# The k^T v product of a linear-attention block: v as the weights, k's softmax divided in place, KV turned by VectorE

## The chip, the cores and the metric

The kernel runs on one core of a Trainium2 chip. The core has five engines that work side by side and wait for each other by semaphores: TensorE (matmuls; in the profile PE, its weight loads PEld), VectorE (DVE), ScalarE (ACT), GpSimd (POOL), and SyncE (SP), which issues most of the transfers. Matmul results land in PSUM, eight banks of 512 fp32 columns on each of 128 partitions; everything else lies in SBUF. The metric is the device time of one execution in microseconds, the median of three timed runs.

## The reference

One transformer block in bfloat16 on 2048 rows of width 640: a linear attention with 32 heads of width 20, then a gated feed-forward layer of width 1536. The part that matters here, cut:

```python
qkv = (x @ wqkv).reshape(B, S, 3, H, Dh)...            # q, k, v per head, Dh = 20
pk = einsum("bhsd,hdf->bhsf", k, w_phi)                # pq from q in the same way
phi_k = concatenate([softmax(pk), softmax(-pk)], -1)   # softmax over the 20 features
kv = einsum("bhsf,bhsd->bhfd", phi_k, v)               # per head, summed over all 2048 rows
z  = einsum("bhsf->bhf", phi_k)
num = einsum("bhqf,bhfd->bhqd", phi_q, kv)
den = einsum("bhqf,bhf->bhq", phi_q, z)[..., None] + 1e-6
o = num / den                                          # then @ wo, residual, feed-forward
```

So each head needs, for each of two signs (the softmax of pk and that of -pk), a 20x20 matrix k^T v and a row z, the sum of phi_k. Nothing of the attention's output can be computed before all 2048 rows of k and v have gone into them.

## The kernel before

The rows are cut into 16 tiles of 128 (a row tile has 128 rows on the partitions). The order of the work on every engine is written out by hand; no scheduler moves anything. Each engine takes its own instructions strictly in the order of the program.

*K phase* (loop over t at line 479, about 17 to 69 us). For each tile: TensorE multiplies the normalised input by the folded k weights (pk, line 288), ScalarE takes exp of pk and of -pk (line 332) into E, a buffer of two halves of 640 columns, one for each sign. TensorE also makes v three tiles ahead (pv), and ScalarE copies it to vS (line 308), where each head has 20 columns of v and a column of ones: the product with the ones gives z. VectorE sums E over each head's 20 features (line 339, `k_norm`) and takes reciprocals rs (line 343). Then v is divided, not k: vt = vS * rs, one instruction for each sign, 128x672 (line 347). The second sign's always runs on GpSimd; the first sign's runs on GpSimd for the tiles listed in `VP` (0, 2, 4, 6, 9, 11, 12) and on VectorE for the others, where it is put off until after the next tile's line 339 (`todo`). There are eight vS buffers, eight E and eight vt.

*k^T v* (`kv_tile`, line 359). The product isn't made tile by tile but in groups, listed in `KVG` and `KVQ`: tiles 0 and 1 in iteration 6, tiles 2 to 5 in iteration 9, tiles 6 to 9 in iteration 13, tiles 10 to 12 in iteration 15 behind the first q products, tiles 13 to 15 after the loop. E is the stationary operand (the weights): for each sign, for each of five chunks of 32 feature columns and each of four quadrants, one weight load of 128x32 and one matmul whose moving operand is vt of the two or three heads that touch the chunk, 42 or 63 columns. The four quadrants are the four blocks of 32 PSUM partitions; matmuls of different quadrants run side by side in the array. That is 40 pairs of weight load and matmul a tile, all adding into one PSUM bank, kvp. As a chunk of 32 features holds parts of two or three heads, the result has blocks that belong to no head.

*The seam* (`kv_mask`, line 370). VectorE adds 0.5e-6 to z (line 372), then multiplies kvp by kmask, which is 1 where a feature row belongs to the head of the column and 0 elsewhere, into KV (line 374). GpSimd builds kmask in iteration 7 (lines 516 to 522), clears KV in iteration 8, and copies kmask into two border columns of KV in iteration 11; SP copies kmask to the other three quadrants with three transfers in iteration 9, ahead of the last load of WqT.

*Q phase* (from line 781). The q products (`q_mm`, line 388; pq, five matmuls of 512 columns for each of 20 chunks) and their exponentials on ScalarE (`q_exp`, line 393, into Eq) are spread over the seam. The attention products (`attn_a`, line 586) use Eq as weights and slices of KV as the moving operand, two or three heads of 22 columns at a time. The first, of tile 0, comes right behind the first half of the fifth q product, and it needs KV. From there each tile goes through VectorE, GpSimd and ScalarE (lines 605 to 640), a transpose oT, the output projection (line 660), a second LayerNorm, and the feed-forward matmuls (lines 720 and 739), which take the rest of the time.

PSUM in this phase is a ring of four double banks (`gtile`); kvp holds one of them from iteration 3 to the seam, and the second q product after the first attention product takes that one over.

## Time and profile before

The three timed runs took 273.31, 273.39 and 273.48 us. The profiled execution of the same program has a span of 272.1 us from its first instruction to its last; what a timed run has beyond that, about 1.3 us, lies before and after.

| what | value |
| --- | --- |
| time, median of 3 runs | 273.39 us |
| span of the profiled execution | 272.1 us |
| TensorE busy | 267.4 us, 98% |
| VectorE / ScalarE / GpSimd busy | 64% / 51% / 37% |
| granted TensorE clock | 0.999 |
| k^T v (line 366) in the chain | 2.2% |
| attention products (line 586) in the chain | 2.3% |
| divisions on GpSimd (line 347) | 23 of 1371 ns |
| divisions on VectorE (line 347) | 9 of 1078 ns |

How to read the lines below: a line of the groups gives source line, engine, operation, output<-inputs, partitions x elements, xcount, then busy time in us and the mean duration of one in ns, then the engine's idle time before them and what ended it. A line of the timeline gives start and length in us, engine, line, operation and count of a run of equal instructions, and in brackets the idle time before it. The length of a run of matmuls includes the last one's way through the array, so the time until the next run's start is what it costs the stream. The chain is the work that ended last, followed back: where it is on TensorE, TensorE was not waiting.

### The profile page before, as it was taken

Reading aid. Unit: us, or ns where it says so; the run is one execution under the profiler, and the core shown is the slowest. Engines: PE = TensorE matmul, PEld = TensorE weight load, DVE = VectorE, ACT = ScalarE, POOL = GpSimd, SP = SyncE. Lnnn points to the kernel's source line nnn. Section 1 sums busy time; section 2 is a strip of 40 time slices with the busy share of each in tenths; the row PEclk is TensorE's granted clock in tenths of the full one; section 3 lists DMA queues with packets and bytes.
Section 4 is the critical chain, followed back from the end, with each engine's and each line's share of the span. In section 5 each row is a group of like instructions: output and inputs, shape, how many; then the busy total and the mean of one; then the engine's idle time right before and its main releaser. Section 6 shows DMA issues by size and latency. Waiting matters only on the chain.

```text
span 272.1 us, 7250 instructions
## 1 busy us (share of the span) xinstructions
PE 267.4 (98%) x2990; PEld 171.9 (63%) x2990; DVE 173.7 (64%) x330; ACT 138.1 (51%) x238; POOL 100.5 (37%) x220
## 2 busy tenths in 40 slices
PE   7999999999999999999999999999999999999996
PEld 6777777765555887788755455675555576444574
DVE  4899999997767766695457874346778332333322
ACT  5669997787789765364624256213345600233100
POOL 4248997877002336374123464003166400000000
PEclk9999999999999999999999999999999999999999
DMA  7987466241676632332202133110222411000011
GB/s 185 213 195 169 69 100 78 51 106 67 224 252 197 197 100 57 75 74 51 57 18 52 25 62 60 48 52 0 51 48 48 52 48 51 24 0 0 2 48 48
DMA packets 45408, 22.11 MB, mean 81 GB/s; under 512 B 37952, under 2 KB 43328, under 8 KB 45376
## 3 DMA queue, kind: packets, MB, share of 16 engines
q1 hardware_dynamic: 44720, 21.64, 33.5%
q8 instruction: 23, 0.38, 0.6%
q10 hardware_dynamic: 656, 0.03, 0.2%
q14 instruction: 9, 0.07, 0.1%
HBM read 10.18 MB, written 2.62 MB: 47 GB/s over the span
## 4 chain that ended last, share of the span: by engine, by line
PE 95%; DMA 2%; ACT 1%; DVE 1%; SPq 0%; issue 0%
PE gu L720 39%; PE pd L739 19%; PE pq L388 8%; PE po L660 8%; PE pk L288 8%; PE pv L288 7%; PE ab L586 2%; PE kvp L366 2%; DMA Wv<-in_A_wqkv_dram 2%; PE wa L240 1%; PE pv L304 1%; ACT vS L308 1%; PE tp L159 0%; DVE LN1T L160 0%; SPq L187 0%
## 5 line engine op out<-in xcount | busy, mean ns | idle before, releaser
L723 ACT ACTIVATE g<-gu 128x512 bf16<-128x512 f32 (+1 forms) x60 | 30.6, 510 | 63.5 <-PE gu L720 62.6
L726 DVE TENSOR_TENSOR GT<-gu,g 128x512 bf16<-128x512 f32 (+1 forms) x60 | 34.3, 578 | 43.8 <-PE gu L720 31.1
L720 PE MATMUL gu<-LN2T,Wg 128*128 128x512 bf16 (+1 forms) x300 | 61.8, 337 | 0.0
L720 PE MATMUL gu<-LN2T,Wu 128*128 128x512 bf16 (+1 forms) x300 | 61.8, 336 | 0.0
L739 PE MATMUL pd<-Wd,GT 128*128 128x320 bf16 (+2 forms) x396 | 53.5, 295 | 0.0
L739 PEld LDWEIGHTS <-GT 128*128 128x128 bf16 x396 | 37.9, 98 | 14.6 <-DVE GT L726 0.2
L720 PEld LDWEIGHTS <-Wu 128*128 128x128 bf16 x300 | 29.4, 98 | 22.6
L720 PEld LDWEIGHTS <-Wg 128*128 128x128 bf16 x300 | 28.6, 98 | 20.3
L288 PEld LDWEIGHTS <-LN1T 128*128 128x128 bf16 x290 | 27.9, 98 | 10.4
L347 POOL TENSOR_TENSOR vt<-vS,rs 128x672 bf16<-128x672 bf16 x23 | 31.0, 1371 | 5.9 <-DVE rs L343 5.7
L742 DVE TENSOR_TENSOR y<-pd,x_sb 128x320 bf16<-128x320 f32 (+2 forms) x29 | 13.9, 480 | 29.4 <-PE pd L739 29.4
L660 PE MATMUL po<-Wo,oT 128*128 128x320 bf16 x160 | 24.5, 299 | 0.0
L288 PE MATMUL pk<-Wk,LN1T 128*128 128x320 bf16 x160 | 24.4, 299 | 0.0
L388 PE MATMUL pq<-LN1T,Wq 128*128 128x512 bf16 x100 | 22.9, 379 | 0.0
L339 DVE TENSOR_REDUCE sk<-E 128x64 f32<-128x1280 bf16 x16 | 22.9, 1429 | 0.0
L393 ACT ACTIVATE Eq<-pq 128x1024 bf16<-128x1024 f32 (+1 forms) x26 | 19.9, 831 | 3.1 <-PE pq L388 3.0
L332 ACT ACTIVATE E<-pk 128x640 bf16<-128x640 f32 x28 | 18.7, 746 | 2.8 <-PE pk L288 2.8
L146 ACT ACTIVATE ln<-x_sb,v,rstd 128x640 bf16<-128x640 bf16 x14 | 12.9, 920 | 14.3 <-POOL v L699 14.2
L660 PEld LDWEIGHTS <-oT 128*128 128x128 bf16 x160 | 15.4, 98 | 6.9 <-ACT oT L160 0.2
L288 PE MATMUL pv<-Wv,LN1T 128*128 128x320 bf16 x130 | 19.8, 299 | 0.0
L635 DVE TENSOR_TENSOR tt<-AB,w 128x1280 bf16<-128x1280 f32 x12 | 17.8, 1486 | 1.0 <-POOL w L628 0.9
L615 POOL TENSOR_TENSOR pr<-AB 128x64 f32<-128x64 f32 x10 | 6.8, 678 | 26.8 <-DVE AB L596 20.7
(114 smaller groups left out, 289.9 us busy)
## 6 DMA issues: line engine op xcount, KB each, us to landing
out_dram<-y SPq DMA_DIRECT2D x15, 160.0 KB, 1.8
x_sb<-in_A_x_dram SPq DMA_DIRECT2D x6, 320.0 KB, 3.4
Wu<-in_B_w_up_dram SPq DMA_DIRECT2D x1, 1920.0 KB, 8.9
Wg<-in_B_w_gate_dram SPq DMA_DIRECT2D x2, 768.0 KB, 5.8
Wd<-in_B_w_down_dram SPq DMA_DIRECT2D x1, 1440.0 KB, 7.8
Wo<-in_A_wo_dram SPq DMA_DIRECT2D x1, 800.0 KB, 4.9
x_sb<-in_A_x_dram SPq DMA_DIRECT2D x4, 160.0 KB, 3.7
Wv<-in_A_wqkv_dram SPq DMA_DIRECT2D x2, 320.0 KB, 5.0
```

The lines of the kernel that those rows point to most:

```text
L288: nc.tensor.matmul(ps[:, u, 0:HD], lhsT=lnT(t, c), rhs=W[:, c, u * HD:(u + 1) * HD], start=(c == 0), stop=(c == NC - 1))
L332: nc.scalar.activation(Ek[t][:, s, :].rearrange("p (u f) -> p u f", u=2), pk[:, :, 0:HD], ACTF.Exp, scale=((lnp[t][2], nrstd[t]) if t in C ...
L339: nc.vector.reduce_sum(sk, Ek[t].rearrange("p s (h f) -> p (s h) f", f=Dh), axis=AX.X)
L347: eng.tensor_tensor(vt[:, s], vS[t % 8], rs[:, s * H:(s + 1) * H, None].to_broadcast([P, H, VC]), ALU.mult)
L388: nc.tensor.matmul(pqs[j][:, i, :], lhsT=Wq2[:, kc, c * P:(c + 1) * P], rhs=LN1T[b][:, kc, :], start=(kc == 0), stop=(kc == NC - 1))
L393: nc.scalar.activation(Eq[j][:, :, s, :], pqs[j][:, 0:len(QG[j])], ACTF.Exp, scale=(1.0, -1.0)[s])
L635: nc.vector.tensor_tensor(tt.rearrange("p s (h f) -> p s h f", f=Dh), num, w[:, :, :, None].to_broadcast([P, 2, H, Dh]), ALU.mult)
L660: nc.tensor.matmul(pos[u], lhsT=st[t][:, c, :], rhs=Wo[:, c, u * HD:(u + 1) * HD], start=(c == 0), stop=(c == NC - 1))
L720: nc.tensor.matmul(gu[i][:, 0:n], lhsT=W[:, c, f * P:(f + 1) * P], rhs=LN2T[b][:, c, a0:a1], start=(c == 0), stop=(c == NC - 1))
L723: nc.scalar.activation(g[:, 0:n], gu[0][:, 0:n], ACTF.Gelu_apprx_tanh)
L726: nc.vector.tensor_tensor(st[b, "g", f][:, a0:a1], gu[1][:, 0:n], g[:, 0:n], ALU.mult)
L739: nc.tensor.matmul(ps, lhsT=st[b, "g", f][:, tl * P:(tl + 1) * P], rhs=Wd[:, f, f0:f1], start=(f == 0), stop=(f == NF - 1))
```

## The change

- In `kv_tile` v becomes the stationary operand and E the moving one. For each head (8 in each of 4 quadrants) one weight load takes 32 columns of v: the head's column of ones, its 20 columns of v, and 11 columns of what follows (the next head's, or a pad of ones behind the last). The moving operand is the head's 20 columns of E of both signs at once, 40 columns, and the output goes to two runs of 20 columns of kvp, 160 apart. That is 32 pairs a tile. The result is transposed: v's columns on the partitions, k's features along the free axis.
- As v is now used undivided, E is divided in place: line 347's product becomes E * rs, 128x640 for each sign. vt and its eight buffers go; vS must live until its k^T v product and gets ten buffers (`NV`). Its column of ones moves from the end to the front. `VP` gains tile 7, which moves one division from VectorE to GpSimd. In the last tile, tile 14's division is issued after tile 15's reciprocal instead of before it.
- `kv_mask` no longer masks. ScalarE (first sign) and VectorE (second sign) each scale one half of kvp, row by row, add a row constant, and write it as bfloat16 into KT, where each head's 20 features stand at the place in the 32-column blocks that its features have in Eq; the rest of KT is zero. Then VectorE transposes KT into KV in blocks of 32x32, one instruction for each sign, 128x384. The factors (sc, bi) are made early by six small GpSimd instructions from the identity matrix.
- kmask goes, with its GpSimd instructions and its three transfers. Clearing KV (528 columns) becomes clearing KT (768).
- KV has 32 columns for each head instead of 22; `attn_a` reads 22 of the 32, starting one column later for the first sign. Numbers and sizes of its matmuls are the same.
- Two of the second half's five q matmuls are issued before the first attention product instead of after it.

```diff
-    VP = (0, 2, 4, 6, 9, 11, 12)
+    VP = (0, 2, 4, 6, 7, 9, 11, 12)
...
+    vF = [p1.tile([P, H * VC + 11], BF16, name=f"vS{i}") for i in range(NV)]
+    vS = [v[:, 0:H * VC].rearrange("p (h f) -> p h f", f=VC) for v in vF]
...
+    for i in range(NV):
+        nc.gpsimd.memset(vF[i][:, H * VC:], 1.0)
...
-        if t - 1 in todo:
+        if t - 1 in todo and t < NT - 1:
             todo.pop(t - 1)()
         rs = small(p1, [P, 2 * H], "rs")
         nc.vector.reciprocal(rs, sk)
-        Vt[t] = vt = ev.tile([P, 2, H, VC], BF16, name="vt", bufs=8)
 
         def mult(s, eng):
-            eng.tensor_tensor(vt[:, s], vS[t % 8], rs[:, s * H:(s + 1) * H, None].to_broadcast([P, H, VC]), ALU.mult)
+            e = Ek[t][:, s, :].rearrange("p (h f) -> p h f", f=Dh)
+            eng.tensor_tensor(e, e, rs[:, s * H:(s + 1) * H, None].to_broadcast([P, H, Dh]), ALU.mult)
 
         mult(1, nc.gpsimd)
         if t in VP:
             mult(0, nc.gpsimd)
         elif t == NT - 1:
+            todo.pop(t - 1)()
             mult(0, nc.vector)
         else:
             todo[t] = lambda: mult(0, nc.vector)
...
-        for s in (0, 1) if t in (0, NT - 1) else (1, 0):
-            for c in range(NC):
-                i, h, n = SLOT[c]
-                for r in range(4):
-                    f0, h0 = r * QF + c * 32, r * QH + h
-                    nc.tensor.matmul(kvp[QUAD[r], s * SL + i:s * SL + i + n, :],
-                                     lhsT=Ek[t][:, s, f0:f0 + 32], rhs=Vt[t][:, s, h0:h0 + n, :],
-                                     start=(s == c == t == 0), stop=(t == NT - 1), skip_group_check=True)
+        E = Ek[t].rearrange("p s (h f) -> p s h f", f=Dh)
+        for i in range(QH):
+            for r in range(4):
+                h = r * QH + i
+                nc.tensor.matmul(kvp[QUAD[r], :, i * Dh:(i + 1) * Dh], lhsT=vF[t % NV][:, h * VC:h * VC + 32],
+                                 rhs=E[:, :, h, :], start=(i == t == 0), stop=(t == NT - 1), skip_group_check=True)
 
     def kv_mask():
-        nc.vector.tensor_scalar_add(kvp[:, :, Dh], kvp[:, :, Dh], 0.5e-6)
-        dst = bass.AP(KV.tensor, KV.offset, [KV.ap[0], [SL * KC + 1, 2], [KC, SL], [1, VC]])
-        nc.vector.tensor_tensor(dst, kvp.rearrange("p (s h) f -> p s h f", s=2),
-                                kmask[:, None, :, None].to_broadcast([P, 2, SL, VC]), ALU.mult)
+        for s in range(2):
+            dst = bass.AP(KT.tensor, KT.offset + s * SL * 32, [KT.ap[0], [Dh + 32, QH], [1, Dh]])
+            src = kvp[:, s].rearrange("p (h f) -> p h f", f=Dh)
+            if s == 0:
+                nc.scalar.activation(dst, src, ACTF.Identity, bias=bi[:, 0:1], scale=sc[:, 0:1])
+            else:
+                nc.vector.tensor_scalar(dst, src, sc[:, 1:2], bi[:, 1:2], op0=ALU.mult, op1=ALU.add)
+        for s in range(2):
+            nc.vector.transpose(KV[:, s].rearrange("p n j -> p (n j)"), KT[:, s])
...
+    d = ident.rearrange("p (r j) -> p r j", r=4)
+    nc.gpsimd.tensor_tensor(row[:, 1:3], d[:, 0:2], d[:, 2:4], ALU.add)
+    nc.gpsimd.tensor_tensor(row[:, 0], row[:, 1], row[:, 2], ALU.add)
+    for s, j in ((0, VC + 1), (1, 0)):
+        nc.gpsimd.tensor_scalar(sc[:, s:s + 1], row[:, 0, j:j + 1], -1.0, 1.0, op0=ALU.mult, op1=ALU.add)
+        nc.gpsimd.tensor_scalar(bi[:, s:s + 1], row[:, 0, VC:VC + 1], 0.5e-6, row[:, 0, j:j + 1],
+                                op0=ALU.mult, op1=ALU.add)
...
-        if t == 9:
-            for r in (1, 2, 3):
-                nc.sync.dma_start(kmask[QUAD[r]], kmask[QUAD[0]])
...
-                                     rhs=KV[q, s, i:i + n].rearrange("p h f -> p (h f)"),
+                                     rhs=KV[q, s, i:i + n, 1 - s:1 - s + KC],
...
     q_mm(q, (0,))
+    q_mm(q, (1,), (0, 1))
     attn_a(0, 1)
-    q_mm(q, (1,))
+    q_mm(q, (1,), (2, 3, 4))
     q_exp(q)
```

More of the change, by code (lines that the diff above doesn't have):

```diff
@@ L66 @@
     ST = {0: (8,), 2: (10, 12), 4: (14,)}
-    SLOT = [(c, 3 * c // 2, 2) if c % 2 == 0 else (6 + 3 * (c // 2), 3 * (c // 2) + 1, 3) for c in range(NC)]
+    SLOT = [(5 * (c // 2) + 2 * (c % 2), 3 * (c // 2) + c % 2, 2 + c % 2) for c in range(NC)]
     SL = 12
+    NV = 10
     x_v = A_x.rearrange("b (p t) d -> p (b t) d", t=NT)
@@ L87 @@
     Wu = const.tile([P, NC, FF], BF16, name="Wu")
-    KV = const.tile([P, 2, SL, KC], BF16, name="KV")
+    KT = const.tile([P, 2, SL * 32], BF16, name="KT")
+    KV = const.tile([P, 2, SL, 32], BF16, name="KV")
+    row = const.tile([P, 3, 32], F32, name="row")
+    sc = const.tile([P, 2], F32, name="sc")
+    bi = const.tile([P, 2], F32, name="bi")
     Eq = [const.tile([P, len(g), 2, 512], BF16, name=f"Eq{j}") for j, g in enumerate(QG)]
@@ L92 @@
     hmask = const.tile([P, NC, 8], BF16, name="hmask")
-    kmask = const.tile([P, SL], BF16, name="kmask")
     BD = const.tile([P, NC, 8, Dh], BF16, name="BD")
@@ L172 @@
     Wk2 = p1.tile([P, NC, D], BF16, name="Wk2")
-    vS = [p1.tile([P, H, VC], BF16, name=f"vS{i}") for i in range(8)]
+    vF = [p1.tile([P, H * VC + 11], BF16, name=f"vS{i}") for i in range(NV)]
+    vS = [v[:, 0:H * VC].rearrange("p (h f) -> p h f", f=VC) for v in vF]
     fp_cm = tc.tile_pool(name="fp", bufs=1, side="right", reuse_waits="tile")
@@ L205 @@
     ones = nc.const_aps.tensor(1.0, [P, 512], BF16)
-    for i in range(8):
-        nc.vector.memset(vS[i][:, :, Dh], 1.0)
+    for i in range(NV):
+        nc.vector.memset(vS[i][:, :, 0], 1.0)
     make_identity(nc, ident)
@@ L215 @@
                                 compare_op=ALU.is_ge, fill=0.0, base=Dh - 1 - off, channel_multiplier=-1)
+    for i in range(NV):
+        nc.gpsimd.memset(vF[i][:, H * VC:], 1.0)
     wu = gtile("wu")
@@ L251, in fold @@
                 nc.vector.tensor_copy(dst, src)
-    lnp, Ek, Vt = {}, {}, {}
+    lnp, Ek = {}, {}
     CT = (0, 1)
@@ L307, in v_ev @@
     def v_ev(t):
-        nc.scalar.activation(vS[t % 8][:, :, 0:Dh].rearrange("p (u h) f -> p u h f", u=2),
+        nc.scalar.activation(vS[t % NV][:, :, 1:VC].rearrange("p (u h) f -> p u h f", u=2),
                              pv[t][:, :, 0:HD].rearrange("p u (h f) -> p u h f", f=Dh), ACTF.Copy,
@@ L480 @@
         if t == T3:
-            kvp = gtile("kvp")[:, 0, 0:2 * SL * VC].rearrange("p (h f) -> p h f", f=VC)
+            kvp = gtile("kvp")[:, 0, 0:2 * QF].rearrange("p (s f) -> p s f", s=2)
         late = t in (1, 4)
@@ L514 @@
             ln_ap(0, on_act=True)
-        if t == 7:
-            nc.gpsimd.memset(kmask[QUAD[0]], 1.0)
-            for k, lo, n, base in ((3, 0, 2, 0), (2, 6, 3, 12)):
-                m = kmask[QUAD[0], lo:lo + 6].rearrange("p (k n) -> p k n", k=k)
-                nc.gpsimd.affine_select(out=m, in_=m, pattern=[[4, k], [-Dh, n]],
-                                        compare_op=ALU.is_ge, fill=0.0, base=base, channel_multiplier=1)
-                nc.gpsimd.affine_select(out=m, in_=m, pattern=[[-4, k], [Dh, n]],
-                                        compare_op=ALU.is_ge, fill=0.0, base=Dh - 1 - base, channel_multiplier=-1)
-        if t == 8:
-            nc.gpsimd.memset(KV, 0.0)
-        if t == 9:
-            for r in (1, 2, 3):
-                nc.sync.dma_start(kmask[QUAD[r]], kmask[QUAD[0]])
-        if t == 11:
-            nc.gpsimd.tensor_copy(KV[:, 0, :, KC - 1], kmask)
-            nc.gpsimd.tensor_copy(KV[:, 1, :, 0], kmask)
+        if t == 8:
+            nc.gpsimd.memset(KT, 0.0)
         if t == 13:
```

## The prediction

> **What bounds the kernel now.** I read the page's busy shares and its chain first, then the groups of instructions, then the timeline around each k^T v group.

> ```profile
> span 272.1 us, 7250 instructions
> PE 267.4 (98%) x2990; PEld 171.9 (63%) x2990; DVE 173.7 (64%) x330; ACT 138.1 (51%) x238; POOL 100.5 (37%) x220
> ...
> PE 95%; DMA 2%; ACT 1%; DVE 1%; SPq 0%; issue 0%
> ```

> TensorE is busy from 7 us to the end and almost the whole chain is its own. So a microsecond taken from TensorE's stream is a microsecond off the end, unless a new wait takes its place; work of other engines counts only where TensorE waits for it. The span is 272.1 us; the timed runs (273.31 to 273.48, median 273.39) hold 1.3 us more around it, which the change doesn't touch. I sum on the span and add to the median.

> The k^T v product is line 366, here by shape, then the row of its divisions on VectorE:

> ```profile
> L366 PE MATMUL kvp<-vt,E 128*32 128x42 bf16 x384 | 6.3, 187 | 0.0
> L366 PE MATMUL kvp<-vt,E 128*32 128x63 bf16 x256 | 6.0, 196 | 0.0
> ...
> L347 DVE TENSOR_TENSOR vt<-vS,rs 128x672 bf16<-128x672 bf16 x9 | 9.7, 1078 | 0.1
> ```

> Durations overlap here, so I price by starts. Timeline of TensorE, groups of 80, 160 and 120 matmuls and what follows each:

> ```profile
> 31.36 0.84 PE L366 MATMUL kvp<-vt,E 128*32 128x42 bf16 x80
> 32.16 1.52 PE L288 MATMUL pv<-Wv,LN1T 128*128 128x320 bf16 x10
> ...
> 54.34 1.52 PE L366 MATMUL kvp<-vt,E 128*32 128x42 bf16 x160
> 55.80 1.53 PE L288 MATMUL pk<-Wk,LN1T 128*128 128x320 bf16 x10
> ```

> 80 pairs of weight load and matmul take 0.80 us until the next work, 160 take 1.46: 8.25 ns a pair and 0.14 us for entering and leaving. In the steady part single starts lie 8.3 ns apart in rounds of 42 columns and of 63 alike: the pair costs, not its columns.

> **Fewer pairs.** 40 pairs a tile become 32 (8 heads by 4 quadrants, 40 columns each), in all 640 to 512. At 8.25 ns a tile saves 66 ns, sixteen save 1.06 us. Bounds for the new pair: 7.2 ns (line 586: 40 pairs, 0.40 us with 0.11 for the switch) and, if a column written in pieces cost double, 40 columns like 80, 17 beyond the 63 that are free today: 7 ns per round of four, 128 rounds, +0.9 us. I take 8.25, because column count has shown no effect. Not all of the 1.06 arrives, because of two waits.

> **Tile 5.** Tiles 2 to 5 are one group:

> ```profile
> 39.70 1.31 POOL L347 TENSOR_TENSOR vt<-vS,rs 128x672 bf16<-128x672 bf16 x1
> 40.34 1.40 DVE L347 TENSOR_TENSOR vt<-vS,rs 128x672 bf16<-128x672 bf16 x1
> 40.40 1.70 PE L366 MATMUL kvp<-vt,E 128*32 128x42 bf16 x160
> 42.03 0.45 PE L288 MATMUL pv<-Wv,LN1T 128*128 128x320 bf16 x2
> ```

> VectorE's division of tile 5 ended at 41.73, 0.72 us after GpSimd's current one; its divisions begun at 45.46, 48.64 and 63.67 also end 0.72 us after one of GpSimd's. Matmul 141 of the group started at 41.79, after a gap of 0.21: today only the tile's last 20 wait for VectorE. In the change every product takes both signs, so the whole tile waits. TensorE comes at 40.40-0.13 (tiles 0 and 1), does three tiles (96 x 8.25 = 0.79) and stands at 41.06. The divisions shrink from 672 to 640 columns: VectorE gains 0.03 on each of two earlier ones, GpSimd's three in a row end near 40.77 instead of 41.02, VectorE's at 40.77+0.69, TensorE resumes at 41.51, needs 32 pairs and the exit (0.37), and the next work starts at 41.88 against 42.03. Six tiles have gained 0.15, not 0.40. VectorE has hardly been idle since 18 us, so TensorE's earlier arrival can't hurry it.

> **Tiles 6 to 15.** 80 pairs less, 0.66 us. Their divisions come in time: GpSimd takes over tile 7 (one more of 1.23 us, beside 1.3 us of dropped mask work), VectorE loses 1.45 us at 45.46 and runs ahead, and tile 12, the nearest, was ready at 61.23 for 61.74 and now comes over a microsecond earlier. Sum so far -0.81.

> **The seam after tile 15.** KV must be finished before the first attention product (line 586).

> ```profile
> 67.68 1.14 PE L366 MATMUL kvp<-vt,E 128*32 128x42 bf16 x120
> 68.75 1.25 PE L388 MATMUL pq<-LN1T,Wq 128*128 128x512 bf16 x5
> 69.96 0.46 PE L586 MATMUL ab<-KV,Eq 32*128 32x44 bf16 x40
> ...
> 68.53 1.09 ACT L393 ACTIVATE Eq<-pq 128x512 bf16<-128x512 f32 x2
> ...
> 68.91 0.19 DVE L372 TENSOR_SCALAR kvp<-kvp 128x24 f32<-128x24 f32 x1 [2.38 <-PE kvp L366]
> 69.13 0.68 DVE L374 TENSOR_TENSOR KV<-kvp,kmask 128x504 bf16<-128x504 f32 x1
> ```

> VectorE makes KV in 0.9 us today, hidden by five q products: ready at 69.81, used at 69.96, no stall. In the change the chain has four links. ScalarE scales one half, queued behind the two exponentials that end at 69.62 (successive ones overlap by 0.11): start 69.50. [...] Times before the shift of 0.6 us that all of these share, because the exponentials wait for q products:

> - ScalarE, 128x160: 0.30 at the copies' rate (455 ns at 352 columns, 746 at 704), 0.52 from line 146 with the same two per-row operands (920 ns at 640 columns, less 480 x 0.83). I take 0.52: end 70.02.
> - VectorE, 128x160 from PSUM: 0.19 (line 372, 24 columns) to 0.33 (that plus 136 x 1.06, slope of its copies). I take 0.33, begun at 70.06: 70.39.
> - Transposes: no row. Fastest near: line 264, 640 columns in 386 ns, pro rata 0.25. Line 339 reads 1280 in 1429 ns, one a cycle and 0.1: 0.50. [...] I take 0.50, an instruction that reads each element once. Overlapping by 0.08 as neighbours do: 70.81 and 71.23; TensorE at 71.28.

> TensorE's cover: tiles 13 to 15 end at 67.68+1.07-0.20 = 68.55, five q products and the switch 1.21, the two moved ahead 0.43: 70.19, second half of the attention products 70.34. Stall 71.28-70.34 = 0.94 us. Without those two it would be 1.37.

> [...]

> **At nothing.** Two more memsets on VectorE (0.17) and ten on GpSimd (about 0.1 each) fall into waits of 1.30 and 1.81 us before 5.5 us. Six small GpSimd operations (about 1.9 us from rows of 0.22 to 0.68) fall into its idle 9.97 to 12.11; if late, they delay tile 4's LayerNorm by some 0.3 of the 1.3 us between its transpose's landing (13.48+2.9) and its use at 17.69. The queue of SP loses three mask transfers (2.66 us), and the WqT loads behind them only come sooner. Ten v buffers are reused after tiles that TensorE has done just before. Moving two q products costs tile 0's attention chain 0.43 of the 1.3 us between oT's landing (74.93+2.6) and its use at 78.86; the Wu load, issued behind oT on SP, slips 0.56 of the 2.4 us between its landing (76.83+8.9) and its use at 88.17. The strided KV slices have 44 and 66 columns as before: nothing, or up to 2.4 us over sixteen tiles if each column cost double.

> **Sum.** -0.15 -0.66 +0.94 = +0.13: 273.5 us, no change beyond the 0.2% (0.55 us) that a measurement of this kernel can tell.

> **Rivals.**
> 1. Faster: the seam is short. ScalarE 0.30 and transposes 0.25 leave a stall of 0.22; sum -0.59, 272.8 us. For: sources are small; the compact bf16 form runs fast on line 264. Against: line 146's price, and a transpose isn't a plain copy. Chance 0.15.
> 2. Slower: the transposes are dear. Place: VectorE between the last k^T v product and line 586. Each 0.1 us on both costs 0.2; from 0.71 each it is slower by over 0.55. [...] For: no row excludes it; against: streaming rows. Chance 0.12.
> 3. Slower: matmuls with operands in pieces cost more. Outputs are now two runs of 20 columns, 160 apart; all of before's are one run. If columns double, +0.9 on the sum, 274.4 us, more if KV's slices count too. For: nothing here shows such a form. Against: 42 and 63 columns cost the same, so half as much again is free. Chance 0.13. [...]

> A freer VectorE is worth nothing by itself: TensorE waits for it only at tile 5.

> **Chances.** Forecast 0.57 (its own range 273.0 to 273.9), rivals 0.15, 0.12, 0.13, other losses 0.03. So faster 0.15, same 0.57, slower 0.28. The range reaches to both sides' cases: 272.8 to 274.5.

> **What would show it.** Line 373's matmuls: 512, 8.3 ns between starts; more than 10 is rival 3. A gap near 0.45 us inside the second k^T v group. ScalarE's and VectorE's KT instructions one behind the other, transposes near 0.50, and TensorE idle about 0.9 us before its first attention product; under 0.3 is rival 1, over 1.5 rival 2. I am wrong too if TensorE stands anywhere else, above all before line 664 (oT late) or in the first 18 us.

## The result, and the profile after

The changed kernel takes 274.55 us (median of five runs, 274.31 to 275.63); the kernel before took 273.39 beside it (273.01 to 273.88). The ratio is 1.0056, with a 95% interval of 1.0045 to 1.0067: slower by 1.2 to 1.8 us. Forecast were 273.5 us, with a range of 272.8 to 274.5, and no measurable change as the likeliest case. The profiled execution has a span of 272.8 us against 272.1.

The page of the changed kernel, its first line, busy shares, instruction queue and chain:

```profile
span 272.8 us, 6984 instructions
...
PE 265.3 (97%) x2843; PEld 170.4 (62%) x2862; DVE 174.3 (64%) x332; ACT 138.3 (51%) x239; POOL 100.7 (37%) x230
...
q8 instruction: 22, 0.36, 0.5%
...
PE 73%; DVE 1%; issue 0%; ACT 0%
```

TensorE is busy for 2.1 us less than before (267.4), and yet the end comes later: what was saved has become waiting. (Part of the 2.1 is only missing from the records: 2843 matmuls are listed for 2862 weight loads, and 13 of line 724, worth 0.6 us, are among the missing.) The third line tells of a queue that no transfer of the kernel is issued to. The page calls it `instruction`; in the trace it carries 22 blocks of 16384 bytes. It will matter.

The groups of the new product, by shape, and of the transposes:

```profile
L373 PE MATMUL kvp<-E,vS 128*32 128x40 bf16 x512 | 5.3, 185 | 0.8 <-issue 0.7
...
L386 DVE STREAM_TRANSPOSE KV<-KT 128x384 bf16<-128x384 bf16 x2 | 1.0, 552 | 0.0
```

The pairs are as cheap as was thought. What is new is "issue": 0.7 us in which TensorE waited for nothing that the profile shows. TensorE's waits between 30 and 72 us name two places, and no others:

```profile
PE ab L590 <- DVE KV L386: 0.9, 1, 0.9
PE kvp L373 <- issue: 0.7, 1, 0.7
```

TensorE's timeline shows where. First the third group, tiles 6 to 9 (before: 160 matmuls at 54.34 without a gap):

```profile
53.46 1.22 PE L373 MATMUL kvp<-E,vS 128*32 128x40 bf16 x124
55.35 0.20 PE L373 MATMUL kvp<-E,vS 128*32 128x40 bf16 x4 [0.66 <-issue]
55.48 1.53 PE L295 MATMUL pk<-Wk,LN1T 128*128 128x320 bf16 x10
```

Matmul 124 starts at 54.50 and matmul 125 at 55.35: TensorE starts nothing for 0.85 us (0.66 by the idle time, which counts from the modelled end), although the data of all four tiles has long been there: GpSimd's divisions for tile 9 were done by 51.4. Then the seam, TensorE first, then ScalarE and VectorE:

```profile
67.20 0.94 PE L373 MATMUL kvp<-E,vS 128*32 128x40 bf16 x96
68.07 1.69 PE L399 MATMUL pq<-LN1T,Wq 128*128 128x512 bf16 x6
70.62 0.68 PE L590 MATMUL ab<-KV,Eq 32*128 32x44 bf16 x40 [0.87 <-DVE KV L386]
...
69.00 0.51 ACT L382 ACTIVATE KT<-kvp,bi,sc 128x160 bf16<-128x160 f32 x1
...
69.55 0.44 DVE L384 TENSOR_SCALAR KT<-kvp,sc,bi 128x160 bf16<-128x160 f32 x1 [3.42 <-ACT KT L382]
69.90 1.03 DVE L386 STREAM_TRANSPOSE KV<-KT 128x384 bf16<-128x384 bf16 x2
```

The chain has the four links that the forecast gave it. TensorE stands 0.87 us ahead of the first attention product, and the attention group lasts 0.61 us until the next work instead of 0.40, because its second half waits for the second transpose (a gap of 0.23 us between the starts of matmuls 20 and 21).

Starts of TensorE's groups, after minus before, give the sum. The two first groups (tiles 0 to 5) gain 0.39 us, the third loses 0.56, the last two gain 0.36, the seam costs 1.13 (with the 0.43 of the moved q products left out), and 0.25 comes in small pieces behind it: +1.19, against 1.16 between the medians. (The profiled execution also began 0.53 earlier, because its first Wv transfer landed earlier; that is left out here. The prediction's 1.3 us around the span was too small for it: every run whose time and span are both listed has 1.66 to 1.85, so the profiled execution of the kernel before, at 272.1, was itself some 0.4 us slower than the median.)

### The profile page after: what moved, and what is told of

Read it like the earlier page. It is cut to its first block, busy times and chain, and to the rows that moved or that the text cites. A ratio compares the mean times of both kernels' runs of the same rounds, so it can differ in the third digit from the quotient of the medians.

```text
span 272.8 us, 6984 instructions
## 1 busy us (share of the span) xinstructions
PE 265.3 (97%) x2843; PEld 170.4 (62%) x2862; DVE 174.3 (64%) x332; ACT 138.3 (51%) x239; POOL 100.7 (37%) x230
## 4 chain that ended last, share of the span: by engine, by line
PE 73%; DVE 1%; issue 0%; ACT 0%
PE gu L724 38%; PE pd L743 19%; PE po L664 8%; PE pq L399 5%; PE ab L590 2%; DVE KV L386 0%; PE tp L163 0%; DVE KT L384 0%; ACT KT L382 0%; DVE y L746 0%
## 5 line engine op out<-in xcount | busy, mean ns | idle before, releaser
L354 POOL TENSOR_TENSOR E<-E,rs 128x640 bf16<-128x640 bf16 x24 | 30.2, 1288 | 6.5 <-DVE rs L350 4.0
```

The costliest lines, as they stand in the source:

```text
L354: eng.tensor_tensor(e, e, rs[:, s * H:(s + 1) * H, None].to_broadcast([P, H, Dh]), ALU.mult)
```

## The experiments

**Is the stall in the third group a matter of instructions?** The trace's transfers on the instruction queue suggest it: one block of 16384 bytes (22 of them came for the 5724 instructions of TensorE's 2862 weight loads and their matmuls, by estimate one for some 260; the stalls below will turn out to lie multiples of 256 apart) came at 52.70 to 54.15, across the start of that group; in the kernel before the block had come at 48.57 to 49.97, over 4 us ahead of it. Counting instructions through TensorE's program, the group begins with number 1226 (before: 1322), and it stops behind number 1473, which is 63 short of 1536 = 6 x 256. If that is the cause, instructions that do nothing useful, put far ahead, must move the stall. The tiny matmuls added here write to the scratch bank of the warm-up; nothing reads them.

```diff
+    def tiny(n):
+        for i in range(n):
+            nc.tensor.matmul(wu[QUAD[i % 4], 1, 0:32], lhsT=ones[:, 0:32], rhs=ones[:, 0:32], start=True, stop=True)
...
-    warm(*[512] * 2, *[P] * 28)
+    warm(*[512] * 2, *[P] * 20)
+    tiny(56)
```

> The changed kernel with 48 more instruction pairs ahead of everything: 8 of the 28 warm-up matmuls of 128 columns give way to 56 tiny ones (32 columns, 32 weights). The work itself is the same; only the place of each instruction in TensorE's program moves on, by 96. Theory (instruction blocks): the 0.85 us in the third k^T v group is a wait for the next block of 256 instructions (16384 bytes), whose transfer began only 0.8 us before the group. With 96 more instructions ahead the third group lies in the program where it lay before the change (1322 instead of 1226), the transfer starts about 6 us ahead of it, and the stall is gone: no gap over 0.1 us in that group, time 0.85 us below the changed kernel, about 273.7. Rival (something in the data, the weights or PSUM at that place of the group): the gap of 0.66 ahead of matmul 125 stays, time unchanged at about 274.5.

```diff
-    warm(*[512] * 2, *[P] * 28)
+    warm(*[512] * 2, *[P] * 28)
+    tiny(4)
```

> The changed kernel with 4 more tiny instruction pairs (8 instructions) behind the warm-up. Instruction blocks: the stall begins 4 pairs earlier in the third group, ahead of matmul 121 instead of 125, and is shorter by about 0.5 us, because the transfer is asked for 8 instructions earlier, at a time when TensorE passes some 15 instructions in a microsecond: about 0.3 us left of 0.85. Rival (data, weights or PSUM): the gap stays ahead of matmul 125, at 0.66 idle.

```diff
-    warm(*[512] * 2, *[P] * 28)
+    warm(*[512] * 2, *[149] * 16, *[150] * 8)
```

> The changed kernel with 4 warm-up pairs fewer (24 matmuls of 149 or 150 columns instead of 28 of 128, the same columns in all). Instruction blocks: all 128 matmuls of the third group run through, the stall comes right behind them, ahead of the pk products of line 295, and is longer by about 0.5 us: 1.4 us against 0.85, the time longer by as much. Rival (data, weights or PSUM): the gap stays ahead of matmul 125, at 0.66 idle.

TensorE's timeline, of 4 pairs more:

```profile
53.57 1.19 PE L378 MATMUL kvp<-E,vS 128*32 128x40 bf16 x120
55.73 0.23 PE L378 MATMUL kvp<-E,vS 128*32 128x40 bf16 x8 [0.97 <-issue]
```

Of 4 pairs fewer:

```profile
54.81 1.25 PE L373 MATMUL kvp<-E,vS 128*32 128x40 bf16 x128
57.45 0.84 PE L295 MATMUL pk<-Wk,LN1T 128*128 128x320 bf16 x5 [1.39 <-ACT ln L150]
```

And of 48 pairs more:

```profile
53.61 1.25 PE L378 MATMUL kvp<-E,vS 128*32 128x40 bf16 x128
54.80 1.53 PE L300 MATMUL pk<-Wk,LN1T 128*128 128x320 bf16 x10
```

The stall stands behind 124 matmuls, behind 120 with 8 instructions more ahead, behind all 128 with 8 fewer, and not there at all with 96 more. Wherever it came, it is behind number 1473 of the program; no data, weight or bank goes with it. (The name ACT ln in the second of these is only the event that came last.) By starts, as the expectations count it, the stall was about as long as expected for 4 pairs fewer (1.4, measured 1.57) and not for 4 more (0.3, measured 1.16): the transfer there began no earlier against the group (52.83 for 53.57; 52.70 for 53.46) and took 1.62 us. Each of these two kernels ran once, in 276.02 us (4 more) and 276.46 (4 fewer), 1.5 and 1.9 above the changed kernel's median; the longer stall is only 0.3 and 0.7 of that. The first also waited 0.8 us for oT, the transposed attention output, and the second 0.6 for ScalarE at 25 us (what may lie behind both comes below); the rest wasn't taken apart.

The same was asked of the kernel before.

```diff
-    warm(*[512] * 2, *[P] * 28)
+    warm(*[512] * 2, *[P] * 20)
+    tiny(58)
...
     warm(*[P] * 4)
+    tiny(30)
```

> The kernel before, with 80 more instruction pairs (10 warm-up matmuls fewer, as 8 of 28; 58 tiny ones behind the warm-up and 30 behind the second warm-up). Its third k^T v group (160 pairs of the old product) then begins at instruction 1482 of TensorE's program instead of 1322, which is 202 beyond a multiple of 256, as 1226 is in the changed kernel. Instruction blocks: the old product shows the stall too, behind 124 of the 160 matmuls, 0.3 to 1 us long, and it ends 1.2 to 1.3 us after the block's transfer. Rival (the stall belongs to the new product: its weights, strided operands or PSUM writes): the 160 matmuls of the old product run through without a gap.

(The edit takes out 8 warm-up matmuls, not 10, and adds 88 tiny ones.)

TensorE's timeline of it:

```profile
40.26 1.37 PE L371 MATMUL kvp<-vt,E 128*32 128x42 bf16 x141
42.19 0.31 PE L371 MATMUL kvp<-vt,E 128*32 128x42 bf16 x19 [0.57 <-issue]
...
54.74 1.23 PE L371 MATMUL kvp<-vt,E 128*32 128x42 bf16 x124
56.87 0.44 PE L371 MATMUL kvp<-vt,E 128*32 128x63 bf16 x36 [0.90 <-issue]
...
71.41 0.46 PE L592 MATMUL ab<-KV,Eq 32*128 32x44 bf16 x39
72.62 0.19 PE L592 MATMUL ab<-KV,Eq 32*128 32x44 bf16 x1 [0.76 <-issue]
```

The old product stalls too, behind 124 of 160 as expected, a second time behind 141 in the group before, and the attention products stall behind 39 of 40: numbers 1729, 1217 and 2497, each 63 short of a multiple of 256. This kernel ran once, in 276.71 us. So the stall isn't the new product's, nor k^T v's alone; the change only moved the program against the blocks. The ends of the stalls settle what is waited for. Times in us, from the trace's packets and TensorE's starts:

| kernel | block's transfer | TensorE resumes | later by |
| --- | --- | --- | --- |
| changed | 52.70 to 54.15 | 55.35 | 1.20 |
| changed, KT on VectorE (below) | 52.94 to 53.90 | 55.16 | 1.26 |
| changed, q products back (below) | 52.51 to 54.02 | 55.41 | 1.39 |
| changed, 4 pairs more | 52.83 to 54.45 | 55.73 | 1.28 |
| changed, 4 pairs fewer | 55.07 to 56.03 | 57.45 | 1.42 |
| before, 80 pairs more | 39.59 to 40.90 | 42.19 | 1.29 |
| before, 80 pairs more | 54.54 to 55.49 | 56.87 | 1.38 |
| before, 80 pairs more | 70.32 to 71.24 | 72.62 | 1.38 |

In all eight stalls TensorE goes on 1.20 to 1.42 us after the block's transfer, whenever that was. With the changed kernel's 21 other blocks no such wait shows: its waits name "issue" once, 0.7 us. With 128x320 matmuls TensorE passes some 15 instructions in a microsecond (ten pairs from 55.48 to 56.85), so 256 of them last about 17 us, an estimate by that rate. A group of k^T v passes 256 in 1.06 (128 pairs at 8.25 ns).

**A second cost of the same blocks.** The kernel with 48 pairs more had no stall in the group and was still slower: 276.7 us (276.05 to 277.44), ratio 1.0123 (1.0102 to 1.0144). TensorE's waits of it name the new place:

```profile
PE po L669 <- DMA oT<-o: 1.9, 2, 1.4
PE ab L595 <- DVE KV L391: 0.9, 1, 0.9
```

oT is brought by a transposing transfer of 672 packets (640 of 256 bytes, 32 of 4), in the changed kernel's trace within 0.84 us from 95.11 on. Here 670 came between 94.40 and about 95.2, and the last two, of 4 bytes each, at 96.5, just when an instruction block (95.58 to 96.54) had passed. Only a shift of the program was tried on it:

```diff
-    warm(*[512] * 2, *[P] * 20)
-    tiny(56)
+    warm(*[512] * 2, *[P] * 18)
+    tiny(74)
```

> The changed kernel with 64 more instruction pairs ahead instead of 48. With 48 the stall in the k^T v group was gone, but TensorE stood 1.42 us at 97.6 and 0.46 at 128.4 for the transposed attention output oT, and the last two packets of 4 bytes of the transfer that brought oT came at 96.5, when a block of instructions (16384 bytes, 95.58 to 96.54) had passed, 1.3 us behind the others. Theory (an instruction block under way holds back the end of a transposing transfer): 16 pairs more bring that block 1.7 us earlier, ahead of the transfer's last packets, and the other one at 125.21 too; both gaps go (under 0.2 us), and the k^T v group stays free of a stall. Rival (oT is late for another reason that the warm-up brings with it, such as the data's own lateness or SP's queue): the gap of 1.4 us at 97.6 stays.

It ran once, in 275.61 us. The wait at 128.4 is gone. The other is not, but is down to 0.54:

```profile
PE po L669 <- DMA oT<-o: 0.5, 1, 0.5
```

The block came only 1.36 us earlier against the work, not 1.7, and so met the first half of the transfer: block 95.30 to 96.32, oT's packets 95.48 to 97.22, twenty of them taking 0.97 to 1.13 us where the median takes 18 ns. The expected clean escape failed.

That a transposing transfer is held back when an instruction block passes, all the traces bear out. From 70 us on, the 672-packet transfers that stand alone (no other such packets within 1.35 us) took 0.83 to 1.24 us where no block met them, 238 of them, and 1.44 to 2.39 us where one did, 17 of 17. Two of the 17 are in the changed kernel's own trace: the transfer of 169.14 to 170.93, whose last two packets, of 4 bytes, came at 170.90, at the end of a block (169.94 to 170.91) and over 0.8 us behind the others; and that of 212.40 to 214.25, of which twenty packets took 0.90 to 1.18 us, beside a block of 212.07 to 213.29. How the block does it is not shown: the traces name no DMA engine for a packet, and in the run above the held packets ended 0.7 us after the block. The kernel with 4 pairs fewer probably shows the same: a transposing LN1T transfer issued at 13.03, whose issue lasted 2.42 us instead of 1.21, beside a block at 13.57 to 15.04. It put ScalarE and then TensorE a microsecond late.

**The seam.** The chain begins with ScalarE, whose half waits behind exponentials while VectorE is idle for 3.42 us.

```diff
-            if s == 0:
-                nc.scalar.activation(dst, src, ACTF.Identity, bias=bi[:, 0:1], scale=sc[:, 0:1])
-            else:
-                nc.vector.tensor_scalar(dst, src, sc[:, 1:2], bi[:, 1:2], op0=ALU.mult, op1=ALU.add)
+            nc.vector.tensor_scalar(dst, src, sc[:, s:s + 1], bi[:, s:s + 1], op0=ALU.mult, op1=ALU.add)
```

> The changed kernel with both halves of KT made by VectorE (line 384's instruction twice, none on ScalarE), so that the seam no longer waits for ScalarE's exponentials. Theory (the chain of four links, begun late by ScalarE): VectorE starts at 68.23 instead of 69.55, the two halves and the two transposes at 0.35, 0.35, 0.48 and 0.55 end at 69.96, TensorE's cover ends at 69.75, and the second half of the attention products is covered 0.2 us longer: a stall of about 0.05 instead of 1.13, the time 1.05 us below the changed kernel, about 273.5. Rival (the transposes, or the way from VectorE to TensorE, are what TensorE waits for, whatever the start): less than 0.4 us is won, 274.15 or more. The stall in the third k^T v group stays at 0.85 in either case.

VectorE's and TensorE's timelines of it:

```profile
68.07 0.80 DVE L381 TENSOR_SCALAR KT<-kvp,sc,bi 128x160 bf16<-128x160 f32 x2 [1.73 <-PE kvp L373]
68.78 1.03 DVE L383 STREAM_TRANSPOSE KV<-KT 128x384 bf16<-128x384 bf16 x2
...
67.05 0.94 PE L373 MATMUL kvp<-E,vS 128*32 128x40 bf16 x96
67.92 1.69 PE L396 MATMUL pq<-LN1T,Wq 128*128 128x512 bf16 x6
69.53 0.65 PE L587 MATMUL ab<-KV,Eq 32*128 32x44 bf16 x40
```

The idle time is gone; from the last group's start to the end of the attention group TensorE needs 3.06 us instead of 4.03, so 0.97 of the 1.13 came back (1.05 expected). The time is 274.2 us, ratio 1.0025 (1.0013 to 1.0037) against 1.0056: 0.85 us less, within the intervals what the profile says, though not the 273.5 that was expected of the median. The transposes cost what they did; it was when the chain began that counted. Inside the attention group 0.19 us is left of the wait for the second transpose.

The other half of the seam's account, the q products moved ahead:

```diff
     q_mm(q, (0,))
-    q_mm(q, (1,), (0, 1))
     attn_a(0, 1)
-    q_mm(q, (1,), (2, 3, 4))
+    q_mm(q, (1,))
```

> The changed kernel with the two q products put back behind the first attention product. Theory (the seam's end is set by ScalarE's start and the three links behind it): KV comes at the same time, TensorE arrives 0.43 us earlier and stands 1.30 us instead of 0.87 ahead of its first attention product; time 0.43 above the changed kernel, about 275.0. Rival (the order is worth nothing, because tile 0's attention chain starts later for it and gives the time back): within 0.15 of 274.55.

```profile
70.68 0.68 PE L590 MATMUL ab<-KV,Eq 32*128 32x44 bf16 x40 [1.30 <-DVE KV L386]
```

TensorE stands 1.30 us, as expected, and the time is 275.03 (ratio 1.0071, 1.0057 to 1.0084). The 0.43 us of work that TensorE had in hand shortened its wait by as much (0.87 for 1.30).

**Grouping.** Tiles can also be grouped so that neither tile 5 nor the block is waited for.

```diff
-    KVG = {6: (0, 1), 9: (2, 3, 4, 5), 13: (6, 7, 8, 9)}
-    KVQ = {0: (10, 11, 12)}
+    KVG = {6: (0, 1), 9: (2, 3, 4), 12: (5, 6, 7, 8)}
+    KVQ = {0: (9, 10, 11, 12)}
```

Alone:

> The changed kernel with the new grouping alone (tiles 2 to 4, 5 to 8, 9 to 12), ScalarE's half of KT as in the change. Theory (the losses are separate and add): the gap at tile 5 (0.3) and the stall for the instruction block (0.3 to 0.85) go, the wait of 0.49 ahead of the first q product comes, the seam stays at 0.87 of idle time; time 0.3 to 0.7 below the changed kernel, 273.9 to 274.2. Rival (the seam grows by what the groups win, because ScalarE's exponentials set it): within 0.15 of 274.55.

With both KT halves on VectorE:

> The changed kernel with both halves of KT on VectorE, as in the run before, and the groups of k^T v cut anew: tiles 2 to 4 in iteration 9, 5 to 8 in iteration 12, 9 to 12 behind the first q product, 13 to 15 at the end. Tile 5 is no longer waited for, and the group of 256 instructions that stalled now begins at instruction 1106 instead of 1226, about 100 ahead of the point where the next block is asked for. Theory (three separate losses: tile 5's division 0.3, the instruction block 0.3 to 0.85, the seam 1.1): no gap of TensorE over 0.15 us is left behind 7 us, and the time is 0.6 to 1.1 below the run with VectorE alone, 273.1 to 273.6, under the kernel before (273.4) or level with it. Rival (the losses move on: a new wait in another group, or a transposing transfer that meets an instruction block): the time stays within 0.3 of 274.2.

Alone it took 274.82 us (ratio 1.0055, 1.0040 to 1.0070), no gain: a miss. The stall and tile 5's wait went, the seam's 0.87 stayed, 0.48 came ahead of the first q product as expected there, and 0.38 more ahead of the first feed-forward product, for a LayerNorm transfer (LN2T). Of its packets 18 took over 0.8 us, from 86.26 on, like those that a block held back; but no block was near, the last having ended at 84.81. So a block seems not to be the only thing that holds such a transfer back, and the cause here stays open. With VectorE it took 273.49 (1.0017, 1.0000 to 1.0033), and TensorE's timeline shows the one gap left:

```profile
56.04 1.52 PE L295 MATMUL pk<-Wk,LN1T 128*128 128x320 bf16 x10
58.04 2.32 PE L396 MATMUL pq<-LN1T,Wq 128*128 128x512 bf16 x10 [0.49 <-ACT E L339]
```

The first q product takes the bank that ScalarE's exponentials of iteration 14 leave; they end at 57.99. The group in iteration 13 had covered them, and it was no longer there. (The gap lies behind the same 732 matmuls of the program as the stalls at number 1473, but by chance: the block for that place had come at 51.22 to 52.15, almost 6 us earlier.) So the groups were cut once more, 5 and 6 in iteration 12, 7 to 9 in iteration 13:

```diff
-    KVG = {6: (0, 1), 9: (2, 3, 4), 12: (5, 6, 7, 8)}
-    KVQ = {0: (9, 10, 11, 12)}
+    KVG = {6: (0, 1), 9: (2, 3, 4), 12: (5, 6), 13: (7, 8, 9)}
+    KVQ = {0: (10, 11, 12)}
```

> As the run with both halves of KT on VectorE and the groups cut anew, but tiles 5 to 8 cut into 5 and 6 in iteration 12 and 7 to 9 in iteration 13, and 10 to 12 behind the first q product. There TensorE had stood 0.49 us ahead of the first q product for ScalarE's exponentials of iteration 14, because iteration 13 had no k^T v group left to cover them. Theory (the group in iteration 13 was that cover): with 96 pairs there again (0.8 us) the gap goes, one more group costs 0.14 us, and no stall for an instruction block comes, as 85 slow instructions lie between the block's request and the group's end; no gap over 0.15 us behind 7 us, time 0.35 below that run, 273.1, which is 0.1% under the kernel before. Rival (the wait belongs to ScalarE's own lateness, or the block's stall comes back at the 92nd pair of that group): a gap of 0.3 or more at one of these places, time 273.4 or more.

It takes 272.77 us (median of eleven), ratio 0.9985 (0.9973 to 0.9998): faster than both kernels, than the one before by 0.4 us (0.05 to 0.75, an interval that barely excludes no gain). It is 0.8 below the run above, where 0.35 was expected; its one gap of 0.49 and the group's price explain the 0.35 alone. The gap is gone; the timeline of TensorE where it was:

```profile
53.72 0.96 PE L373 MATMUL kvp<-E,vS 128*32 128x40 bf16 x96
...
56.32 1.52 PE L295 MATMUL pk<-Wk,LN1T 128*128 128x320 bf16 x10
57.68 2.32 PE L396 MATMUL pq<-LN1T,Wq 128*128 128x512 bf16 x9
```

Last, whether the moved q products are still worth something there:

> The kernel of the run beside it, with the two q products put back behind the first attention product. Its seam has five q products (1.07 us and the switch) against VectorE's chain of 1.73 us from the end of k^T v to the second transpose. Theory (the chain sets the seam): the second half of the attention products then comes 0.43 us earlier than KV allows, and TensorE stands about 0.3 us more, 0.3 us above the run beside it. Rival (the chain is covered by five q products too): no difference over 0.1.

```profile
68.90 0.68 PE L587 MATMUL ab<-KV,Eq 32*128 32x44 bf16 x40 [0.33 <-DVE KV L383]
```

They are: 273.52 us (ratio 1.0008, 0.9998 to 1.0018), 0.6 us more by the ratios, with intervals of 0.25 to each side. By the traces the two kernels need 3.06 and 3.07 us from the last group's start to the end of the attention group, this one with 0.43 us less done in it: 0.33 is idle time, 0.05 a slower attention group (0.62 for 0.57), whose second half waits for the second transpose.

## Why the prediction was wrong

- **Fewer pairs: right.** 512 matmuls came, at 7.9 to 8.0 ns between starts, 8.25 priced. Rival 3 is dead: outputs in two runs of 20 fp32 columns cost nothing that shows (the median between starts is 8.0 ns in both kernels). Its 7 ns for 17 columns is an estimate by the 216 ns between starts of the 512-column matmuls of line 388; at that rate 40 columns one behind the other would be 17 ns apart, so 8.0 also shows the four quadrants at work side by side. The strided KV slices cost nothing either (0.40 us a group in both kernels).
- **Tiles 0 to 5: -0.15 forecast, -0.39 measured.** TensorE did stand for tile 5's division, but for about 0.2 to 0.3 us instead of 0.45, hardly more than the 0.21 of the kernel before: VectorE's division of that tile ended at 40.79, which is 41.3 when the earlier beginning of this execution is taken out, where 41.46 was forecast.
- **Tiles 6 to 15: -0.66 forecast, +0.20 measured.** This is the step that failed. Without the 0.85 us in the third group it would be -0.65, the forecast itself. "Not all of the 1.06 arrives, because of two waits" left out a third, which hangs on no engine and no datum: with 96 instructions fewer ahead of the group, the next instruction block came across the start of the densest stretch of the program (52.70 to 54.15, the group from 53.46 on; before 48.57 to 49.97, for 54.34). The runs that move the stall by moving the program, and that bring it into the old product, show this. The text had named the sign ("wrong too if TensorE stands anywhere else"), but no price.
- **The seam: chain right, +0.94 forecast, +1.13 measured.** ScalarE's link came as priced (0.51 for 0.52). VectorE's half took 0.44 instead of 0.33, and the two transposes 1.03 together, begun one behind the other, against 0.92 by 0.50 each with their overlap. Rival 1 and rival 2 are dead, with 0.55 us for a transpose where rival 2 began at 0.71. The forecast's 0.50 was an estimate from line 339's 1429 ns for 1280 elements (less 0.1, for 384 of them, plus 0.1); how long a cycle of VectorE is, no trace shows. That VectorE's half starts behind ScalarE's (70.06 behind 70.02 in the forecast) the trace bears out: 69.55 behind 69.51, with 3.42 us idle before. Why it has to, no run shows.
- **At nothing: right** for GpSimd, SP, the small operations and the moved q products' effect on later chains; TensorE waits nowhere in the first 18 us for them, nor at line 664. (It waits 0.51 us for VectorE at 4.86, but only because its warm-up ended earlier; the work behind that wait began 0.10 us sooner than before.) The moved products are worth the 0.43 that they were given, by the idle time.
- **The sum** of the forecast's terms with 0.85 for the stall, 0.19 more for the seam and 0.24 less for the first tiles is +0.93; what is left to +1.16, about 0.2 us, lies in the small pieces behind the seam, which no run took apart.

## What to carry to other kernels

A saving in a dense stretch of small instructions moves the whole program behind it against its instruction blocks. Count the instructions: where some 250 of them run within about 2.5 us (an estimate by the transfers and stalls here: 0.9 to 1.7 us for a block, 1.20 to 1.42 behind it), find where multiples of 256 fall (here the stalls stood 63 ahead of them), and read "issue" in the waits as a question about instructions. And before a chain is split over two engines, look which of them is free when it can begin: here the idle one alone was 0.97 us faster than the two, and the wait between them ate what the split could bring.
